# Fixed insertion plans for unit lists and row gathers, and two column groups for the last 64 undecided units

## The chip, the cores and the metric

One core of one Trainium2 chip runs the whole program: a block-recurrent cross attention whose output goes into a switch top-1 mixture of experts. The metric is the device time of the program in microseconds. Times inside the program (us from the start of the span) are those of one profiled execution.

## The reference, cut to what matters

```python
# attention: B=8, H=8, S=512, Ns=32, D=64
scores = scale * x @ state.T;   a  = softmax(scores);   xread = a @ state      # 512 token rows a batch
scores2 = scale * state @ x.T;  a2 = softmax(scores2);  sread = a2 @ x         # 32 state rows a batch
x = concat([xread, sread]) -> (B * (S + Ns), H * D) = (4352, 512)
# switch: E=8 experts, D=512, F=1024
expert_idx = argmax(x @ w_gate);  gate_w = softmax(x @ w_gate)[expert_idx]
out[rows of e] = gate_w * (relu(x[rows of e] @ w1[e]) @ w2[e])
```

Everything is float32.

## The kernel before, in words

The 512 token rows of a batch are taken to go to one expert, guessed from the mean of its states (table `eb`). A token row is a convex mixture of 32 state rows, so the kernel multiplies the states by w1 first (`states_w1` makes G, 32 x 1024 for each head) and bounds how far a token can lie from their mean. From that bound, `lists(b)` (7 steps) divides the 1024 hidden units of batch b in three kinds: units that are positive for every token (up to CAPP = 512; their relu does nothing, so they enter as one product M, matmuls `pm`), undecided units (up to CAPU = 192, as a group of 128 and one of 64; matmuls `phu`, relu into `hu`), and units that are never active, which are dropped.

A list goes this way. PE turns G (`pgt`), ACT copies it to `gt`, DVE takes statistics (`bn`) and computes row numbers (`nn` to `to`). POOL scatters the columns of G to their places in a DRAM table `g_dram` by 8 indirect DMAs. `fetch(b)` reads the sorted table back into `gp` by 3 DMAs, and `gather` fetches the matching rows of w2 by 6 indirect DMAs into `w2c`. `mask(b)` on DVE zeroes the places beyond the list's ends in `gp`. Then `batch(b)` runs on PE: `pgu` (turns the undecided units), `pm` (M), `phu`, and `py` in two pairs of chunks; ACT scales and stores. Batch 0 doesn't use lists: `in_full` computes all 1024 units.

The state rows (256, in two halves t = 0 and 1) are sorted by expert (`sort_states(t)`: matmuls `psT`, `pls`, `prs`, then about 41 small DVE instructions on 128x8 tables, here the sort chain) and computed in 3 rounds of 128 rows (`rounds`: the rows `xg` are read back from DRAM by POOL, then `ptx`, `pgh` twice, `pth`, `pgy` twice; weights come through a ring of 5 buffers of 0.786 MB, loaded four at a time).

Every engine runs its instructions in the order in which the program writes them. The order between the strands is set at insert points: `in_full` has 24 of them, and `batch` 13 (one behind `pgu`, four in `pm`, one behind each `phu`, three in each pair of `py`). A string at each point says which generators take a step: B `back` (second half of attention), T `front` (scores), S `lists`, F `fetch`, M `mask`, R the state rows, K late constants. Before, a generator whose turn came too early waited by its own `while ...: yield`; the list of batch b + 1 was scattered during batch b; fetch and its 6 gathers came together at insert point 10 of batch b (it needs `summed[0]`, set behind the last `pm`), and the mask right behind. The table `g_dram` was held twice, in turn.

Names in the rows and traces: every operation is recorded by one helper and so has the line L51; tiles tell them apart. A program matmul in float32 shows as two records.

Of the kernel before, what the change touches and what calls it, by code (L numbers as in the profile page):

```python
# [20 lines left out]
def kernel(  # L21
# [68 lines left out]

    st_dram = dram.tile([B * NS, DM], FP32)
    ss_dram = [dram.tile([NR * 128, XW], I32, name=f"ss_dram{t}") for t in range(NT)]
    g_dram = [dram.tile([CAPP + CAPU, GW], FP32, name=f"g_dram{i}") for i in range(2)]

    pa = ps_a.tile([128, 4, 512], FP32, name="pa")
    pc = pa[:, :, 0:256]
# [63 lines left out]
    gp.memset(blank2[:, DM + 1:DM + 2], FAR)  # L160

    def clear():
        for i in range(2):
            for r in range(0, CAPP + CAPU, 128):
                n = min(128, CAPP + CAPU - r)
                sp.dma_start(out=g_dram[i][ds(r, n)].bitcast(I32), in_=blank[0:n, 0:GW])
        for t in range(NT):
            for r in range(NR):
                sp.dma_start(out=ss_dram[t][ts(r, 128)], in_=blank2[:])
# [295 lines left out]
    def lists(b):  # L465

        G = new_G()
        w1t = w1s.pop(b)
        for k in range(2):
            states_w1(w1t, stT[:, 0, b], G, k)  # L470
            if k == 1 and b + 1 < B:
                load_next_w1(b + 1)
            yield
        gt = ffn.tile([128, NFC, GW], FP32, tag="gt", name="gt")
        dve.tensor_scalar(gt[:, :, GW - 1:GW].bitcast(I32), pos8[:].unsqueeze(2), e_at[:, b:b + 1], None, ALU.add)
        bn = ffn.tile([128, NFC, 2, 3], FP32, tag="bn", name="bn")
# [37 lines left out]
        for f in range(NFC):  # L514
            d = gp.indirect_dma_start(
                out=g_dram[b % 2][:], out_offset=bass.IndirectOffsetOnAxis(ap=to[:, f:f + 1], axis=0),
                in_=gt[:, f, :], in_offset=None, bounds_check=CAPP + CAPU - 1, oob_is_err=False)
            tc.declare_no_dep(d.ins, group=f"g{b}", reason="every unit has a row of its own")
            tc.add_to_no_dep_group(f"g{b}", d.ins)
        yield  # L520

    def fetch(b):

        t = gps[b] = ffn.tile([128, NP + NU, GW], FP32, tag="gp", bufs=2, name="gp")
        gp.dma_start(out=t[:, 0:NP + 1], in_=g_dram[b % 2][0:CAPP + 128].rearrange("(j p) k -> p j k", p=128))
        for u in range(2):
            gp.dma_start(out=t[ts(u, 64), NP + 1], in_=g_dram[b % 2][ds(CAPP + 128, 64)])
        w2cs[b] = []
        gather(b, NP + NU)

    def gather(b, n):
        rows = moe_w2.rearrange("e f d -> (e f) d")
# [20 lines left out]
    def batch(b, insert):  # L553
# [18 lines left out]
        for u in range(NU):  # L572
            ph = bank(name="phu")
            for g in range(2):
                pe.matmul(ph[:], lhsT=Gu[:, g, u, :], rhs=tokens_of(a)[:, g], start=(g == 0), stop=(g == 1))
            relu(hu[u][:], ph[:])
            insert()
        store = store_batch(b)
        for c0 in range(0, NC, 2):
# [5 lines left out]
                pe.matmul(py[i][:], lhsT=hu[0][:, ts(c0 + i, 128)], rhs=w2c[NP][:], start=False, stop=False)  # L585
                insert()
            for i in range(2):
                pe.matmul(py[i][:], lhsT=hu[1][ts(i, 64), ts(c0 + i, 128)], rhs=w2c[NP + 1][ts(i, 64)],
                          start=False, stop=True)
            for i in range(2):  # L590
                store(c0 + i, py[i])
# [187 lines left out]
    def late_constants():  # L779
# [2 lines left out]
        dve.tensor_copy(out=wt[:, 1:, 0], in_=eb[:, 1:])  # L782
        dve.tensor_tensor(wt[:, 1:, 1], eb[:, 1:], eb[:, 0:B - 1], ALU.not_equal)
        yield
        dve.tensor_scalar(U128[:], colf[:], iota_p[:, 0:1], None, ALU.is_gt)
        tmp = const.tile([128, 1], FP32)
        quad = const.tile([128, 1], FP32)
# [8 lines left out]
        dve.scalar_tensor_tensor(slot_u[:, 1:2], iota_p[:], 128.0, tmp[:], ALU.add, ALU.add)  # L796
        yield

    attended, done, summed, listed, fetched, turned = [0], [0], [0], [0], [0], [-1]

    def backs():
        for b in range(B):
            while done[0] < b - 3 or b not in soft:
                yield
            for _ in back(b):
                turned[0] = b
                yield
            attended[0] = b + 1

    def fronts():  # L810
        for b in range(1, B):
            for i, _ in enumerate(front(b)):
                yield
                while i == 1 and turned[0] < b - 1:
                    yield

    def listing():
        for b in range(1, B):
            for i, _ in enumerate(lists(b)):
                while (i == 5 and bounded[0] < b) or (i == 6 and fetched[0] < b - 2):  # L820
                    yield
                yield
            listed[0] = b
            yield

    def fetching():
        for b in range(1, B):
            while listed[0] < b or done[0] < b - 1 or summed[0] < b - 1:
                yield
            fetch(b)  # L830
            fetched[0] = b
            yield

    def masking():
        for b in range(1, B):
            while fetched[0] < b:
                for k in "BTSF":
                    next(todo[k], None)
            mask(b)
            yield  # L840

    def tokens():
        for t in range(NT):
# [25 lines left out]
    rest = ["S", "T", "B", "", "F", "B", "SBT", "ST", "SB", "SSM", "T", "ST", "S"]
    pieces = {1: (9, 10, 11, 12, 13), 2: (1, 6, 7, 12), 3: (3, 4, 8, 10, 13), 4: (4, 8, 9, 13),  # L870
              5: (9, 10, 11, 12, 13), 6: (1, 5, 6, 11), 7: (2, 3, 8)}
    for b in range(1, B):
        done[0] = b
        batch(b, inserts([k + "R" * pieces[b].count(i + 1) for i, k in enumerate(rest)]))
    for k in "BTSFMR":
        for _ in todo[k]:
            pass
# [133 lines left out]
```

## Time and profile before

| | |
|---|---|
| time, median of 3 runs | 451.41 us (444.86 to 452.32) |
| the profiled execution, its own time | 448.62 us |
| its span | 446.8 us |
| PE busy | 368.7 us, 83% |
| DVE busy | 206.2 us, 46% |
| ACT and POOL busy | 124.2 and 124.4 us, 28% each |
| DMA moved | 93.46 MB, mean 209 GB/s |

A row of the timeline gives the start, the length, the engine, the operation with output and inputs, and in brackets how long the engine was idle ahead of it and what it waited for. A matmul's form reads rows*columns of the array; 128*32 is one of four column groups. PEclk is the granted clock, 1.00 for the upper of the two levels and 0.50 for the lower. Batches begin at their `pgu`: 1 at 99.8, 2 at 148.2, 3 at 193.4, 4 at 251.4, 5 at 302.0, 6 at 346.4, 7 at 396.4.

### The profile page before, as it was taken

To read this page: it belongs to the slowest core of one execution; us is meant where nothing else is said; L and a number is where in the kernel's file an instruction comes from. 1 tells how busy PE (TensorE), PEld (TensorE's weight loads), DVE (VectorE), ACT (ScalarE), POOL (GpSimd) and SP (SyncE) were. 2 spreads that over 40 slices of the span, in tenths; PEclk is the share of its full clock that TensorE was granted. 3 is DMA by queue.
4 is the path that set the end of the run, shared out by engine and by line. 5 is a ranking of instruction groups with operands and counts; after the bars stand their busy time and mean duration, and the time that the engine had idled before them with its cause. 6 is when DMAs were issued, how large, how long until landed. Compare 5 with 4: busy or idle time off the path is not lost.

```text
span 446.8 us, 9127 instructions
## 1 busy us (share of the span) xinstructions
PE 368.7 (83%) x3288; PEld 168.4 (38%) x3288; DVE 206.2 (46%) x634; ACT 124.2 (28%) x226; POOL 124.4 (28%) x149
## 2 busy tenths in 40 slices
PE   4697999957994799869999699996999749729991
PEld 3443544433442454324523245342534323213330
DVE  4858697367528866490454706345123810010002
ACT  3623524114323341422322322430404211101110
POOL 2000006350155117250161603514073414431000
PEclk9899999986998599997999799997999888958998
DMA  6949982780254459687699944698024665878451
GB/s 182 384 154 252 273 295 70 240 293 28 69 160 130 128 167 292 220 289 269 234 292 377 366 143 139 226 331 301 5 74 134 188 227 213 262 265 254 156 209 76
DMA packets 51346, 93.46 MB, mean 209 GB/s; under 512 B 8583, under 2 KB 19538, under 8 KB 51296
## 3 DMA queue, kind: packets, MB, share of 16 engines
q1 hardware_dynamic: 37792, 61.76, 42.0%
q0 software_dynamic: 8368, 22.65, 15.6%
q10 hardware_dynamic: 5136, 8.41, 5.0%
q8 instruction: 28, 0.46, 0.4%
q14 instruction: 22, 0.18, 0.1%
HBM read 83.40 MB, written 21.15 MB: 234 GB/s over the span
## 4 chain that ended last, share of the span: by engine, by line
PE 32%; DMA 13%; issue 6%; DVE 3%; POOL 3%; ACT 2%; ACTq 0%; POOLq 0%
PE py L51 9%; PE pm L51 7%; DMA w2c<-in_moe_w_dram,gp 5%; PE pgh L51 4%; DMA gp<-g_dram 4%; PE phu L51 4%; PE pgy L51 3%; DMA g_dram<-gt,to 2%; POOL g_dram L51 2%; PE pa L51 1%; DMA xg<-ss_dram 1%; PE pG L51 1%; PE pw L51 1%; ACT y L51 1%; POOL gp L51 0%
## 5 line engine op out<-in xcount | busy, mean ns | idle before, releaser
L51 POOL DMA_INDIRECT g_dram<-gt,to x56 | 56.5, 1010 | 179.5 <-ACT a L51 65.6
L51 PE MATMUL pm<-w2c,gp 128*128 128x512 f32 x112 | 67.4, 745 | 15.6 <-DMA w2c<-in_moe_w_dram,gp 10.5
L51 POOL DMA_INDIRECT w2c<-in_moe_w_dram,gp x42 | 43.8, 1042 | 52.7 <-DMA gp<-g_dram 42.3
L51 PE MATMUL py<-M,aT 128*128 128x512 f32 x112 | 53.8, 603 | 0.0
L51 PE MATMUL py<-w2c,hu 128*128 128x512 f32 (+1 forms) x112 | 44.1, 617 | 0.0
L51 PEld LDWEIGHTS pm<-w2c,gp 128*128 128x128 f32 x112 | 24.0, 234 | 48.7 <-issue 36.5
L51 ACT ACTIVATE y<-py,gw 128x512 f32<-128x512 f32 x32 | 22.0, 689 | 51.1 <-PE py L51 43.4
L51 DVE TENSOR_SCALAR gp<-gp,mk 128x256 f32<-128x256 f32 x42 | 13.0, 367 | 45.8 <-DMA gp<-g_dram 45.7
L51 PEld LDWEIGHTS py<-M,aT 128*128 128x128 f32 x112 | 20.0, 189 | 24.8 <-issue 22.8
L51 PE MATMUL phu<-aT,Gu 128*128 128x512 f32 x56 | 28.4, 635 | 0.0
L51 PE MATMUL pgt<-ident,G 128*128 128x128 f32 x112 | 18.3, 287 | 10.1 <-ACT gt L51 6.1
L51 DVE BATCH_NORM_STATS2 bn<-gt 128x6 f32<-128x256 f32 x56 | 20.6, 412 | 12.4 <-ACT gt L51 12.4
L51 ACT COPY gt<-pgt 128x512 f32<-128x512 f32 x28 | 15.9, 589 | 35.9 <-PE pgt L51 28.2
L51 PE MATMUL pgh<-s,sxT 128*32 128x512 f32 x192 | 23.5, 633 | 1.8 <-ACT gt L51 1.8
L51 DVE TENSOR_SCALAR xs<-pw,s 128x64 f32<-128x64 f32 x16 | 3.8, 279 | 42.9 <-PE pw L51 42.9
L51 DVE COPY G<-pG 128x512 f32<-128x512 f32 x16 | 11.0, 689 | 25.5 <-PE pG L51 25.5
L51 PE MATMUL py<-s,s 128*128 128x512 f32 x48 | 22.5, 598 | 0.0
L51 PEld LDWEIGHTS py<-w2c,hu 128*128 128x128 f32 (+1 forms) x112 | 14.9, 187 | 19.0 <-issue 18.8
L51 PEld LDWEIGHTS pgt<-ident,G 128*128 128x128 f32 x112 | 12.8, 143 | 24.4 <-ACT gt L51 7.7
L51 POOL DMA_DIRECT2D gp<-g_dram x21 | 14.4, 696 | 26.8 <-issue 15.0
L51 PE MATMUL pgy<-s,shT 128*32 128x512 f32 x192 | 21.8, 595 | 0.0
L51 DVE STREAM_TRANSPOSE xt<-x_nat 128x1024 f32<-128x1024 f32 x16 | 19.4, 1228 | 2.4 <-DMA x_nat<-in_x_dram 2.4
(203 smaller groups left out, 473.7 us busy)
## 6 DMA issues: line engine op xcount, KB each, us to landing
s<-in_moe_w_dram SPq DMA_DIRECT2D x144, 256.0 KB
w1t<-in_moe_w_dram SPq DMA_DIRECT2D x8, 2048.0 KB
x_nat<-in_x_dram SPq DMA_DIRECT2D x16, 512.0 KB
out_dram<-y ACTq DMA_DIRECT2D x32, 256.0 KB
gp<-g_dram POOLq DMA_DIRECT2D x7, 642.5 KB, 7.2
ss_dram<-blank SPq DMA_DIRECT2D x8, 257.0 KB
s<-in_moe_w_dram SPq DMA_DIRECT2D x2, 768.0 KB
g_dram<-blank SPq DMA_DIRECT2D x10, 128.5 KB
```

The source lines that it names most:

```text
L51: ins = getattr(self.engine, name)(*args, **kw)
```

## The change

Every insert point now has a written string, in a table per batch (`plans`), and the waiting loops became asserts. Lists are made further ahead: the scatter of list b + 2 stands at insert point 12 of batch b where before that of b + 1 stood in batch b. Fetch and the gathers are three F steps (read the table back; 3 gathers; 3 gathers). One table `g_dram` is left of two. The clearing of the tables moved from before batch 0 behind the first load steps (a K step) and is 6 DMAs less. All rounds of state rows are over by batch 6. Separately, the 64-unit group of `phu`, which was computed 128 wide with each unit twice over 512 tokens (2 program matmuls), is now computed by 4 matmuls of 64 columns and 256 tokens in two column groups, each with half of the chunks, and its relu covers 256 columns instead of 512.

```diff
@@ -160,10 +160,9 @@
     def clear():
-        for i in range(2):
-            for r in range(0, CAPP + CAPU, 128):
-                n = min(128, CAPP + CAPU - r)
-                sp.dma_start(out=g_dram[i][ds(r, n)].bitcast(I32), in_=blank[0:n, 0:GW])
+        for r in range(0, CAPP + CAPU, 128):
+            n = min(128, CAPP + CAPU - r)
+            sp.dma_start(out=g_dram[ds(r, n)].bitcast(I32), in_=blank[0:n, 0:GW])
...
     def fetch(b):
 
         t = gps[b] = ffn.tile([128, NP + NU, GW], FP32, tag="gp", bufs=2, name="gp")
-        gp.dma_start(out=t[:, 0:NP + 1], in_=g_dram[b % 2][0:CAPP + 128].rearrange("(j p) k -> p j k", p=128))
+        gp.dma_start(out=t[:, 0:NP + 1], in_=g_dram[0:CAPP + 128].rearrange("(j p) k -> p j k", p=128))
...
         w2cs[b] = []
-        gather(b, NP + NU)
...
             ph = bank(name="phu")
             for g in range(2):
-                pe.matmul(ph[:], lhsT=Gu[:, g, u, :], rhs=tokens_of(a)[:, g], start=(g == 0), stop=(g == 1))
-            relu(hu[u][:], ph[:])
+                if u < NU - 1:
+                    pe.matmul(ph[:], lhsT=Gu[:, g, u, :], rhs=tokens_of(a)[:, g], start=(g == 0), stop=(g == 1))
+                else:
+                    for i in range(2):
+                        pe.matmul(ph[ts(i, 64), 0:S // 2].rearrange("p (c t) -> p c t", c=NC // 2), lhsT=Gu[:, g, u, ts(i, 64)],
+                                  rhs=a[:, g, i:NC:2].rearrange("p c i t -> p c (i t)"),
+                                  start=(g == 0), stop=(g == 1), skip_group_check=True)
+            n = S if u < NU - 1 else S // 2
+            relu(hu[u][:, 0:n], ph[:, 0:n])
...
-                pe.matmul(py[i][:], lhsT=hu[1][ts(i, 64), ts(c0 + i, 128)], rhs=w2c[NP + 1][ts(i, 64)],
+                pe.matmul(py[i][:], lhsT=hu[1][ts(i, 64), ts(c0 // 2, 128)], rhs=w2c[NP + 1][ts(i, 64)],
...
         dve.tensor_tensor(wt[:, 1:, 1], eb[:, 1:], eb[:, 0:B - 1], ALU.not_equal)
         yield
+        clear()
+        yield
...
     def backs():
         for b in range(B):
-            while done[0] < b - 3 or b not in soft:
+            assert done[0] >= b - 3 and b in soft
+            for i, _ in enumerate(back(b)):
+                turned[0], attended[0] = b, b + i // 3
                 yield
...
     def listing():
         for b in range(1, B):
             for i, _ in enumerate(lists(b)):
-                while (i == 5 and bounded[0] < b) or (i == 6 and fetched[0] < b - 2):
-                    yield
                 yield
-            listed[0] = b
-            yield
+                assert i != 5 or bounded[0] >= b
+                assert i != 6 or fetched[0] >= b - 1
 
     def fetching():
         for b in range(1, B):
-            while listed[0] < b or done[0] < b - 1 or summed[0] < b - 1:
-                yield
+            assert listed[0] >= b and summed[0] >= b - 2
             fetch(b)
             fetched[0] = b
             yield
+            assert done[0] >= b - 1
+            gather(b, 3)
+            yield
+            assert summed[0] >= b - 1
+            gather(b, 3)
+            yield
 
     def masking():
         for b in range(1, B):
-            while fetched[0] < b:
-                for k in "BTSF":
-                    next(todo[k], None)
+            assert fetched[0] >= b
             mask(b)
             yield
...
-    next(todo["B"])
+    for k in "BTT":
+        next(todo[k])
...
     load_next_w1(1)
-    clear()
     in_full(G, aTs[0], w2x, store_batch(0), inserts(
-        "TT,B,TK,BBT,TS,BS,BS,TTS,BS,TS,B,S,TS,T,B,S,BS,TT,F,BS,MTS,BS,TS,S".split(",")))
-    rest = ["S", "T", "B", "", "F", "B", "SBT", "ST", "SB", "SSM", "T", "ST", "S"]
-    pieces = {1: (9, 10, 11, 12, 13), 2: (1, 6, 7, 12), 3: (3, 4, 8, 10, 13), 4: (4, 8, 9, 13),
-              5: (9, 10, 11, 12, 13), 6: (1, 5, 6, 11), 7: (2, 3, 8)}
+        "T,BK,T,TK,BS,B,BS,BB,S,ST,S,S,S,ST,TB,TS,TS,BF,BT,FTS,BST,FSB,TS,TSM"))
+    plans = {
+        1: "SB,SB,S,B,FSBR,STR,STF,SR,TFR,STRM,T,S,BR",
+        2: "B,FS,SR,BTF,SBT,STR,ST,FSR,T,SR,BM,ST,BR",
...
+        6: ",F,R,F,,R,,F,,,M,,",
+        7: ",,,,,,,,,,,,",
+    }
```

On POOL around the end of batch 1 and into batch 2 (ss_dram is the sorted table of state rows, xg the rows read back of it, gp the list read back, w2c the gathered rows of w2), before:

```order
L51 DMA ss_dram_79<-srow,si 512x514
L51 DMA xg<-ss_dram_79 128x514
L51 DMA g_dram_82<-gt,to 704x257 x8
L51 DMA gp<-g_dram_82 128x5x257
L51 DMA gp<-g_dram_82 64x257 x2
L51 DMA w2c<-in_moe_w_dram,gp 128x512 x6
```

and of the change:

```order
L51 DMA ss_dram_79<-srow,si 512x514
L51 DMA g_dram<-gt,to 704x257 x8
L51 DMA xg<-ss_dram_79 128x514
L51 DMA gp<-g_dram 128x5x257
L51 DMA gp<-g_dram 64x257 x2
L51 DMA w2c<-in_moe_w_dram,gp 128x512 x6
```

The read of xg moved from ahead of a list's eight scatters to behind them.

On DVE at the edge from batch 1 to batch 2, where `mk` and `gp` are the masks of batch 2 (nm, sx, sm belong to a softmax, bn to a list's statistics, nn to a list's numbers; in the change `more` ends the sort chain of t = 0), before:

```order
L51 TENSOR_SCALAR mk<-slot_p,nn 128x4
L51 SCALAR_TENSOR_TENSOR mk<-slot_u,nn 128x2
L51 TENSOR_SCALAR gp<-gp,mk 128x256 x6
L51 TENSOR_REDUCE nm<-pa 128x2
L51 TENSOR_SCALAR nm<-nm 128x2
L51 BN_STATS bn<-gt 128x6 x2
L51 TENSOR_REDUCE sm<-sx 128x32
```

and of the change:

```order
L51 TENSOR_SCALAR more<-c_1773 128x1
L51 SCALAR_TENSOR_TENSOR more<-c_1774,more 128x1
L51 TENSOR_SCALAR mk<-slot_p,nn 128x4
L51 SCALAR_TENSOR_TENSOR mk<-slot_u,nn 128x2
L51 TENSOR_SCALAR gp<-gp,mk 128x256 x6
L51 TENSOR_REDUCE sm<-sx 128x32
L51 TENSOR_SCALAR sm<-sm 128x32
L51 RECIPROCAL sm<-sm 128x32
L51 TENSOR_TENSOR sx<-sx,sm 128x1024
L51 COPY nn<-rank 128x2
```

The masks of batch 2 stood ahead of the sort chain, and stand behind it now, with a softmax's second half and the next list's numbers behind them.

On PE at the same edge (pgu opens batch 2; pa_1896 and pa_1902 turn a2 of batch 4; ptx turns xg; prs ranks the state rows), before:

```order
L51 MATMUL pgu<-ident,gp 128x128 x4
L51 LDWEIGHTS U_337
L51 MATMUL prs<-oh,U_337 128x8
L51 LDWEIGHTS ones_b
L51 MATMUL prs<-oh,ones_b 128x8
L51 MATMUL pm<-w2c,gp 128x512 x4
```

and of the change:

```order
L51 MATMUL py<-w2c,hu 128x512 x2
L51 MATMUL pa_1896<-ident,a_1753 128x128 x4
L51 MATMUL pa_1902<-ident,a_1753 128x128 x4
L51 MATMUL pgu<-ident,gp 128x128 x4
L51 MATMUL pw<-x_nat,a2T 32x64 x32
L51 MATMUL pl<-aT,gst 32x128 x8
L51 MATMUL pm<-w2c,gp 128x512 x2
L51 MATMUL pG<-w1t,stT 32x512 x8
L51 MATMUL pm<-w2c,gp 128x512 x2
L51 MATMUL pG<-w1t,stT 32x512 x8
L51 MATMUL ptx<-ident,xg 128x128 x4
```

`prs` moved from behind pgu to well ahead of it (py, rank and the turns of a2 lie between); pw, pl and pG of later batches now lie among the pm, and ptx behind the second of them.

## Rows read from the trace of the kernel before

**Rows 1.** Timeline, PE, 98 to 152: start us, us, work [idle before <-releaser].

```profile
99.77 1.11 PE L51 MATMUL pgu<-ident,gp 128*128 128x128 f32 x4 [4.66 <-DVE cnt L51]
104.20 2.08 PE L51 MATMUL pm<-w2c,gp 128*128 128x512 f32 x2 [3.31 <-ACT gt L51]
...
145.73 1.12 PE L51 MATMUL pgt<-ident,G 128*128 128x128 f32 x4 [6.14 <-ACT gt L51]
...
151.22 0.19 PE L51 MATMUL prs<-oh,U 128*128 128x8 bf16 x1 [1.92 <-DVE oh L51]
```

**Rows 2.** Waits of PE from 190 to 405: us in total, times, longest.

```profile
PE pm L51 <- DMA w2c<-in_moe_w_dram,gp: 10.5, 5, 4.4
PE pgu L51 <- DVE gp L51: 8.7, 2, 8.5
PE ptx L51 <- DMA xg<-ss_dram: 6.2, 1, 6.2
PE prs L51 <- DVE oh L51: 2.9, 1, 2.9
PE pgt L51 <- DVE ys L51: 2.7, 1, 2.7
```

**Rows 3.** Sum of five windows after 190: length, PE busy (granted clock 0.50 in each).

```profile
sum 37.55, PE 27.55; mean PE 5.51
```

**Rows 4.** Timeline, POOL, one list of units (the third).

```profile
168.68 1.00 POOL L51 DMA_INDIRECT g_dram<-gt,to  x1 [6.32 <-DVE r L51]
...
183.80 2.06 POOL L51 DMA_DIRECT2D gp<-g_dram  x3 [4.97 <-issue]
189.13 1.10 POOL L51 DMA_INDIRECT w2c<-in_moe_w_dram,gp  x1 [3.27 <-DMA gp<-g_dram]
...
193.16 1.81 POOL L51 DMA_INDIRECT w2c<-in_moe_w_dram,gp  x1 [0.30 <-PE py L51]
...
196.58 1.00 POOL L51 DMA_INDIRECT w2c<-in_moe_w_dram,gp  x1 [0.30 <-issue]
```

**Rows 5.** Waits of POOL over the whole program.

```profile
POOL g_dram L51 <- ACT a L51: 65.6, 1, 65.6
...
POOL w2c L51 <- DMA gp<-g_dram: 42.3, 8, 9.6
```

**Rows 6.** Timeline, DVE, 107 to 113: second half of one batch's softmax.

```profile
107.99 1.20 DVE L51 TENSOR_REDUCE sm<-sx 128x32 f32<-128x1024 f32 x1
...
111.09 1.25 DVE L51 STREAM_TRANSPOSE aT<-sx 128x1024 f32<-128x1024 f32 x1
```

**Rows 7.** Timeline, DVE, 344 to 359: the masks, then the sort chain's ends.

```profile
344.99 1.95 DVE L51 TENSOR_SCALAR gp<-gp,mk 128x256 f32<-128x256 f32 x6 [4.38 <-DMA gp<-g_dram]
...
351.75 0.14 DVE L51 CAST wi<-prs 128x8 int32<-128x8 f32 x1
...
358.59 0.16 DVE L51 SCALAR_TENSOR_TENSOR more<-c,more 128x1 f32<-128x1 f32 x1
```

**Rows 8.** Timeline, PE, 163 to 241: prices of PE steps at full clock.

```profile
163.40 1.10 PE L51 MATMUL pw<-x_nat,a2T 128*32 128x64 f32 x64
...
175.20 1.09 PE L51 MATMUL pG<-w1t,stT 64*32 64x512 f32 x16
...
217.72 1.98 PE L51 MATMUL phu<-aT,Gu 128*128 128x512 f32 x4
...
237.37 3.64 PE L51 MATMUL pgy<-s,shT 128*32 128x512 f32 x32
```

**Rows 9.** Page, DMA issues: KB each, median us from issue to landing.

```profile
xg<-ss_dram POOLq DMA_DIRECT2D x3, 257.0 KB, 5.0
```

**Rows 10.** Windows by stage: length, busy (x) of PE, PEld, DVE, ACT, POOL, PEclk, DMA, GB/s.

```profile
193.40:251.40 58.00, 49.24 (x442) 20.87 (x441) 27.10 (x70) 16.05 (x29) 16.97 (x18) 0.94 0.87 301
...
396.40:446.80 50.40, 39.05 (x164) 14.10 (x164) 5.46 (x20) 6.79 (x11) 7.12 (x7) 0.87 0.51 171
```

**Rows 11.** Timeline, DVE, 438 to 441: the last of the count behind the rows.

```profile
440.57 0.15 DVE L51 CAST rest_i<-rest_f 128x1 int32<-128x1 f32 x1
```

More of the change, by code (lines that the diff above doesn't have):

```diff
@@ L92 @@
     ss_dram = [dram.tile([NR * 128, XW], I32, name=f"ss_dram{t}") for t in range(NT)]
-    g_dram = [dram.tile([CAPP + CAPU, GW], FP32, name=f"g_dram{i}") for i in range(2)]
+    g_dram = dram.tile([CAPP + CAPU, GW], FP32, name="g_dram")
     pa = ps_a.tile([128, 4, 512], FP32, name="pa")
@@ L515, in lists @@
             d = gp.indirect_dma_start(
-                out=g_dram[b % 2][:], out_offset=bass.IndirectOffsetOnAxis(ap=to[:, f:f + 1], axis=0),
+                out=g_dram[:], out_offset=bass.IndirectOffsetOnAxis(ap=to[:, f:f + 1], axis=0),
                 in_=gt[:, f, :], in_offset=None, bounds_check=CAPP + CAPU - 1, oob_is_err=False)
@@ L519, in lists @@
             tc.add_to_no_dep_group(f"g{b}", d.ins)
+        listed[0] = b
         yield
@@ L524, in fetch @@
         t = gps[b] = ffn.tile([128, NP + NU, GW], FP32, tag="gp", bufs=2, name="gp")
-        gp.dma_start(out=t[:, 0:NP + 1], in_=g_dram[b % 2][0:CAPP + 128].rearrange("(j p) k -> p j k", p=128))
+        gp.dma_start(out=t[:, 0:NP + 1], in_=g_dram[0:CAPP + 128].rearrange("(j p) k -> p j k", p=128))
         for u in range(2):
-            gp.dma_start(out=t[ts(u, 64), NP + 1], in_=g_dram[b % 2][ds(CAPP + 128, 64)])
+            gp.dma_start(out=t[ts(u, 64), NP + 1], in_=g_dram[ds(CAPP + 128, 64)])
         w2cs[b] = []
-        gather(b, NP + NU)
     def gather(b, n):
@@ L802, in backs @@
         for b in range(B):
-            while done[0] < b - 3 or b not in soft:
+            assert done[0] >= b - 3 and b in soft
+            for i, _ in enumerate(back(b)):
+                turned[0], attended[0] = b, b + i // 3
                 yield
-            for _ in back(b):
-                turned[0] = b
-                yield
-            attended[0] = b + 1
     def fronts():
@@ L813, in fronts @@
                 yield
-                while i == 1 and turned[0] < b - 1:
-                    yield
+                assert i != 1 or turned[0] >= b - 1
     def listing():
@@ L819, in listing @@
             for i, _ in enumerate(lists(b)):
-                while (i == 5 and bounded[0] < b) or (i == 6 and fetched[0] < b - 2):
-                    yield
                 yield
-            listed[0] = b
-            yield
+                assert i != 5 or bounded[0] >= b
+                assert i != 6 or fetched[0] >= b - 1
     def fetching():
         for b in range(1, B):
-            while listed[0] < b or done[0] < b - 1 or summed[0] < b - 1:
-                yield
+            assert listed[0] >= b and summed[0] >= b - 2
             fetch(b)
@@ L843, in tokens @@
         for t in range(NT):
-            while attended[0] < 4 * (t + 1):
-                yield
+            assert attended[0] >= 4 * (t + 1)
             yield from sort_states(t)
@@ L851, in inserts @@
     def inserts(plan):
-        steps = iter(plan)
+        steps = iter(plan.split(","))
         def insert():
             for k in next(steps):
-                next(todo[k], None)
+                next(todo[k])
         return insert
-    next(todo["B"])
+    for k in "BTT":
+        next(todo[k])
     G = [sst.tile([128, F], FP32, tag=n, name="G0") for n in ("sh", "shT")]
@@ L865 @@
     load_next_w1(1)
-    clear()
     in_full(G, aTs[0], w2x, store_batch(0), inserts(
-        "TT,B,TK,BBT,TS,BS,BS,TTS,BS,TS,B,S,TS,T,B,S,BS,TT,F,BS,MTS,BS,TS,S".split(",")))
-    rest = ["S", "T", "B", "", "F", "B", "SBT", "ST", "SB", "SSM", "T", "ST", "S"]
-    pieces = {1: (9, 10, 11, 12, 13), 2: (1, 6, 7, 12), 3: (3, 4, 8, 10, 13), 4: (4, 8, 9, 13),
-              5: (9, 10, 11, 12, 13), 6: (1, 5, 6, 11), 7: (2, 3, 8)}
+        "T,BK,T,TK,BS,B,BS,BB,S,ST,S,S,S,ST,TB,TS,TS,BF,BT,FTS,BST,FSB,TS,TSM"))
+    plans = {
+        1: "SB,SB,S,B,FSBR,STR,STF,SR,TFR,STRM,T,S,BR",
+        2: "B,FS,SR,BTF,SBT,STR,ST,FSR,T,SR,BM,ST,BR",
+        3: "B,FS,SBTR,TF,ST,SR,ST,FSR,B,STR,BMT,ST,B",
+        4: "BT,FS,STR,BF,SB,SBR,SB,FSR,R,SR,M,SR,R",
+        5: "R,FS,SR,F,S,SR,S,FSR,,SR,M,S,R",
+        6: ",F,R,F,,R,,F,,,M,,",
+        7: ",,,,,,,,,,,,",
+    }
     for b in range(1, B):
         done[0] = b
[L874 to L877, printed above, removed]
+        batch(b, inserts(plans[b]))
+    for k, left in todo.items():
+        assert next(left, None) is None, k
     others = const.tile([128, B, E], FP32)
```

## The prediction

> **What bounds the kernel now.** I read first where the matmul engine stands idle, then at what clock it works, then what DVE and POOL do just before. PE's timeline shows runs of dense work, and a few long holes where one batch ends and the next begins. At 0→1 it waits 4.66 ahead of pgu and 3.31 ahead of the first pm; at 1→2, 6.14 and 1.92: 8.06 [rows 1]. From 190 to 405 PE's waits by what ended them are 10.5 (gathered rows), 8.7 (masks), 6.2 (xg), 2.9 (route of the state rows) and 2.7 (a state result): 31.0, of which 24.8 without xg's [rows 2]. Each hole is followed by work at half clock. Five windows of it after 190, xg's left out, hold 27.55 of PE work; at full clock that would take half, so they cost 13.8 [rows 3]. The reader is to see that a hole is paid about one and a half times.
>
> What makes those late holes is POOL's chain for one list: 8 scatters (168.68 to about 178.8), 4.97 until the fetch, 2.06 to issue it, 3.27 until its rows are there, 6 gathers from 189.13 to 197.6 [rows 4]. PE opened batch 3 at 193.4 and so met the gathers half done. The chain is serial, about 29 us, and its start is late: before the fetch at point 10 it may not go on.
>
> **The change part by part.** I make the sum against the profiled execution's own time, 448.6, which is 2.8 below the median of 451.4.
>
> *Edges from 2→3 on: −24.8 and −13.8.* A list is scattered a batch ahead of its fetch, the fetch stands at point 2 or 4 of the batch before, the gathers at points 2 to 8, and the mask at point 11. Laid along PE's work by those points, the rows land some 20 us ahead of pgu in batches 3 and 4, 6 to 12 in 5 and 6, and about with it in 7, where I leave 1.5 of waiting (below). A wait for the fetch of 9.6, the longest seen [rows 5], where the list shown has 3.27, would take up what is spare in 5 alone. So the waits on gathers, masks and results go, and the half clock behind them. What hides the chain now is a whole batch of PE work (50 to 58 [rows 10]); if that cover were gone, the old holes would be back. xg's wait in batch 6 I leave in: t = 1's rows are sorted and read back in one go in batch 5 as they were in 6.
>
> *Column groups: −6.0.* A phu group of four records takes 1.98 with the end of its last, so about 0.43 a record, 1.72 in all [rows 8]. With 64 columns and 256 tokens in each half of the array the same product needs half: 0.86 saved in each of 7 batches. That column groups run side by side is seen in this trace: 32 records of pgy, four column groups of 32, take 3.64, where 32 times 0.43 would be 13.8 [rows 8]. Bounds: 0 (one after the other) and 6.0; I take 6.0, since the groups of pgy overlap fourfold. The relu is shorter on an engine that doesn't bind.
> The Trainium skill (TensorEngine Tiling (Array Packing), Key Properties) says that a change of tiling mode drains the engine. Of pgy the row shows 3.64 against 8 times 0.43, 3.44 [rows 8], thus up to 0.2 for a mode's end; two more such changes a batch would take back 7 × 0.4 = 2.8 by that rule, and I leave it out of the sum.
>
> *Batch 0: −2.* The clearing writes no longer stand ahead of the loads of x, and the 3.31 ahead of pm [rows 1] goes, since the rows of list 1 are landed by then. The mask of batch 1 now stands last on DVE behind a softmax, so a wait ahead of pgu stays, 4.66 or more. Bounds −4 (all of it gone but that) and +3 (the softmax steps ahead of the masks, at 1.2 each, all late); I take −2, since the 3.31 is the surer part.
>
> *Edge 1→2: +2.4.* The order on DVE is now: sort chain, masks, softmax end, numbers of list 3, aT; before, the masks were first. The chain is 351.75 to 358.75, 7.0; masks with their two marks 2.35 [rows 7]: 9.35 from prs to pgu, while PE has some 7.1 of py, rank and turns there. That is a wait of 2.4 if the chain starts right at prs and of 6.2 if a list's statistics (13 small steps at about 0.2) and a reduction of 1.2 [rows 6] stand ahead of it; I take 4.4. Then pl waits for aT: four softmax steps 3.0, six numbers 1.0, aT 1.25 [rows 6], 5.2 against 1.6 of PE (pgu and pw [rows 8]), so 3.7. prs itself waits for the route, 1.92 and 2.9 before [rows 1, 2]; 2.4. Together 10.5 in place of 8.06.
>
> *xg in batch 2: +10.* Before, xg was read before the scatters of list 3, and ptx found it there. Now it stands behind them on POOL. From the end of the masks (T): numbers ready T + 4.1; eight scatters of 1.27 (168.68 to 178.83 [rows 4]) end T + 14.4; xg issued and landed (5.0, [rows 9]) T + 20. PE gets to ptx at about T + 11.3 (pl at 5.4 and 0.44 long, then four records of pm twice 1.72, pG twice 1.03 [rows 8]). Wait 8.6, and 1.4 for the clock behind it. Everything on PE after ptx in the batch (pm, pgt, phu) waits with it. Bounds: 5 (the scatters go earlier) and 12.
>
> *Rounds closer together: +3.* The two halves of pgh now stand some 4.3 apart in a batch, with only five ring buffers; a half needs four more, 3.1 MB, which at 301 GB/s [rows 10] is 10.4, from the first release 2.7 before the end of the first half. I take 1 for each of three rounds; bounds 0 and 4.
>
> *Smaller:* scores of batch 7, which stood under the old holes, +2.6 (two softmax steps of 1.20 and 1.25, [rows 6], and their start); prs in batch 5, which I removed with the late edges, comes back, +2.4; the rows of batch 7, +1.5. At the tail, the last state result and a dozen small instructions up to rest_i (440.57 [rows 11]) stand no longer behind the last matmul: a dozen times 0.17 (41 in 7.0 [rows 7]) and one of 0.75, −2.8; bounds 0 and −4.
>
> Sum: −24.8 − 13.8 − 6.0 − 2.0 + 2.4 + 10 + 3 + 2.6 + 2.4 + 1.5 − 2.8 = −27.5, so 421.1. Of PE's small waits of under 0.75 I assume that they stay.
>
> **Rivals.**
> *(a) The forecast*, late edges close and early ones don't: about 421, 407 to 432 by the bounds of its terms.
> *(b) Early edges close too.* The first two edges (4.66 + 3.31 + 8.06 [rows 1]) and the added waits (10 + 2.4 + 3 + 2.6 + 2.4 + 1.5 = 21.9) come from where DVE and POOL stand, by a few microseconds each. If DVE keeps up (it is busy 27 of 58 in the densest stretch [rows 10]) half of these 38 goes, 19, and some 4 of half clock behind it: about 398. Against it: in batch 1 the order on DVE leaves no room.
> *(c) Waits move.* The same transfers now fall into fewer microseconds, and rounds, gathers and lists of three batches share DMA at 0.87 of its time in one stretch already [rows 10]. If each late edge keeps half of its hole (38.6/2), 421.1 + 19.3 = 440. For it: the row of 193 to 251; against it: after batch 5 nothing is left to fetch.
> *(d) The column groups don't run side by side:* 421.1 + 6 = 427, the part of the change that does not do what it says.
> *(e) Slower.* With one table, scatter of list b + 1 may start only behind the fetch of list b, so POOL's chain cannot overlap itself. If the cycle of a list is C, POOL, which starts on its first list near 69 (65.6 of it waiting [rows 5]), ends its last gather near 69 + 7C, and 50.4 of batch 7 follow [rows 10]; that exceeds the span of 446.8 from C = 46.8. At C = 50 the time is 471. From the rows C is 29, with the longest wait 9.6 [rows 5] 35; POOL would have to be held 12 a list longer. It's a little chance.
> *(f) POOL's own issue slows.* One gather took 1.81 where others take 1.00 [rows 4]. If DVE work, denser now, did that to each of the 14 indirect DMAs of a list, 0.8 × 14 = 11 a cycle: it would eat the 6 to 12 that 5 and 6 have spare and come out in full at 7: some 5 and 11, 437.
> The Trainium skill (SBUF — State Buffer, section SBUF: two separate sides) has the rule behind (f): a DVE copy in a two-port mode locks GpSimd out of writing descriptors. [...]
>
> **How the numbers follow.** Chances: (a) 0.50, (b) 0.20, (c) 0.13, (d) 0.08, (e) 0.04, (f) 0.05. The predicted time is that of (a), 421. The range reaches from 394, a little under (b)'s 398 since its half could be more, to (c)'s 440: 394 to 440 leaves out (e), and the ends of (b) and (c), some 2 in 10. (a)'s own range is 407 to 432. About 2% (9 us of 451) is what a measurement of this kernel can tell from no change. Faster by over 2% means under 442.4: (a), (b), (d), (f) and most of (c), 0.88. Within 2%: the rest of (c) and of (f), 0.08. Slower: (e), 0.04.
>
> **What would show it.** In the profile after: no wait of PE for w2c, none of pgu for masks from batch 3 on, no low clock there but around the ptx of the second half; phu's second group at about 0.9; in batch 2 a wait of ptx for xg of 5 to 12, in batch 1 waits of prs, pgu and pl that add to some 10; on POOL a fetch that starts more than 25 before its pgu. Wrong if PE still stops for w2c or masks in batches 4 to 7 (c, e, f), if phu's group takes 1.7 (d), or if ptx in batch 2 finds its rows (b).

## The result, and the profile after

| | before | after |
|---|---|---|
| median | 449.28 us (4 runs, 444.86 to 452.32) | 427.24 us (4 runs, 427.11 to 428.27) |
| ratio to before | | 0.9546, 95% interval 0.9456 to 0.9636 |
| the profiled execution, its own time | 448.62 us | 427.33 us |
| its span | 446.8 us | 425.5 us |

The change is faster by 4.5%; forecast were 421 and a range of 394 to 440. Ratios leave out a run that took over 1.5% more than the fastest of its kernel: here the 452.32, and below one of 441.3 among the runs with later lists. The page of the changed kernel, busy times and the granted clock in 40 slices:

```profile
PE 363.0 (85%) x3316; PEld 166.4 (39%) x3316; DVE 205.4 (48%) x634; ACT 122.5 (29%) x226; POOL 125.0 (29%) x149
...
PEclk9989999996997966999999899999998698999998
```

The span lost 21.3: PE's busy time 5.7 (368.7 to 363.0) and PE's idle time 15.6. PE's waits from 190 on in the changed kernel (us in total, times, longest), the answer to [rows 2]:

```profile
PE ptx L51 <- DMA xg<-ss_dram: 9.3, 1, 9.3
PE phu L51 <- ACT M L51: 3.2, 1, 3.2
PE pgh L51 <- DMA s<-in_moe_w_dram: 2.2, 1, 2.2
...
PE pgy L51 <- DMA s<-in_moe_w_dram: 0.9, 2, 0.7
PE prs L51 <- DVE oh L51: 0.8, 1, 0.8
```

No wait for gathered rows and none for masks is left there; 10.5 and 8.7 stood there before. What is left is a wait for xg, one behind ACT, and waits for the weights of the state rounds, which the kernel before did not have. The long waits one by one, PE's timeline (in brackets the idle time ahead and what it waited for):

```profile
102.01 1.12 PE L51 MATMUL pgu<-ident,gp 128*128 128x128 f32 x4 [8.03 <-issue]
...
135.24 0.19 PE L51 MATMUL prs<-oh,U 128*128 128x8 bf16 x1 [3.23 <-DVE oh L51]
...
152.58 1.08 PE L51 MATMUL pl<-aT,gst 128*32 128x128 f32 x16 [4.45 <-DVE s L51]
...
167.84 1.09 PE L51 MATMUL ptx<-ident,xg 128*128 128x128 f32 x4 [6.67 <-DMA xg<-ss_dram]
...
237.54 1.08 PE L51 MATMUL phu<-aT,Gu 128*64 128x256 f32 x8 [3.23 <-ACT M L51]
...
333.55 1.08 PE L51 MATMUL ptx<-ident,xg 128*128 128x128 f32 x4 [9.27 <-DMA xg<-ss_dram]
```

The first edge costs what it cost (8.03 in one piece, 4.66 + 3.31 before [rows 1]); the second too (3.23 + 0.51 ahead of pgu + 4.45 = 8.19 against 8.06). The two ptx waits stand where xg was put behind a list's scatters on POOL.

### The profile page after: what moved, and what is told of

It is laid out like the page before. It is cut to its first block, busy times and chain, and to the rows that moved or that the text cites. A ratio compares the mean times of both kernels' runs of the same rounds, so it can differ in the third digit from the quotient of the medians.

```text
span 425.5 us, 9174 instructions
## 1 busy us (share of the span) xinstructions
PE 363.0 (85%) x3316; PEld 166.4 (39%) x3316; DVE 205.4 (48%) x634; ACT 122.5 (29%) x226; POOL 125.0 (29%) x149
## 3 DMA queue, kind: packets, MB, share of 16 engines
q1 hardware_dynamic: 36992, 61.04, 44.0%
## 5 line engine op out<-in xcount | busy, mean ns | idle before, releaser
L51 POOL DMA_INDIRECT g_dram<-gt,to x56 | 56.3, 1004 | 177.0 <-DVE to L51 93.8
L51 PE MATMUL py<-M,aT 128*128 128x512 f32 x112 | 58.6, 649 | 0.0
L51 PE MATMUL pm<-w2c,gp 128*128 128x512 f32 x112 | 56.4, 636 | 2.2 <-ACT y L51 1.5
L51 POOL DMA_INDIRECT w2c<-in_moe_w_dram,gp x42 | 44.6, 1062 | 43.7 <-DMA gp<-g_dram 33.1
L51 PEld LDWEIGHTS py<-M,aT 128*128 128x128 f32 x112 | 21.4, 207 | 27.7 <-issue 25.8
L51 PEld LDWEIGHTS pm<-w2c,gp 128*128 128x128 f32 x112 | 20.9, 202 | 28.6 <-issue 23.3
L51 PE MATMUL pgh<-s,sxT 128*32 128x512 f32 x192 | 25.9, 600 | 2.2 <-DMA s<-in_moe_w_dram 2.2
L51 PE MATMUL pgy<-s,shT 128*32 128x512 f32 x192 | 26.1, 596 | 1.5 <-DMA s<-in_moe_w_dram 0.9
L51 PE MATMUL phu<-aT,Gu 128*64 128x256 f32 (+1 forms) x84 | 21.8, 486 | 3.2 <-ACT M L51 3.2
L51 PE MATMUL pa<-xt,stT 32*32 32x128 f32 x1024 | 18.9, 295 | 4.1 <-DVE xt L51 3.2
L51 PE MATMUL pG<-w1t,stT 64*32 64x512 f32 x256 | 19.6, 634 | 0.6 <-DVE G L51 0.6
L51 DVE STREAM_TRANSPOSE sx<-pa 128x256 f32<-128x256 f32 x32 | 11.5, 417 | 17.8 <-PE pa L51 17.8
L51 DVE COPY G<-pG 128x512 f32<-128x512 f32 x16 | 10.9, 688 | 17.3 <-PE pG L51 17.3
```

Source lines behind the costliest of these rows:

```text
L51: ins = getattr(self.engine, name)(*args, **kw)
```

## The experiments

Times are medians of four runs, beside runs of the kernel before on the same chip (450.6 for the first four experiments, 450.3 for the three after them). The changed kernel stood at 427.2 (427.1 to 428.3), and on the chip of those three at 427.4 (424.6 to 429.4). It was not run again beside the first four, where the kernel before took 450.6 for the result's 449.3, so of their differences from it only the 4.4 of the third round lies clear of the scatter.

**The column groups undone.**

```diff
-                if u < NU - 1:
-                    pe.matmul(ph[:], lhsT=Gu[:, g, u, :], rhs=tokens_of(a)[:, g], start=(g == 0), stop=(g == 1))
-                else:
-                    for i in range(2):
-                        pe.matmul(ph[ts(i, 64), 0:S // 2].rearrange("p (c t) -> p c t", c=NC // 2), lhsT=Gu[:, g, u, ts(i, 64)],
-                                  rhs=a[:, g, i:NC:2].rearrange("p c i t -> p c (i t)"),
-                                  start=(g == 0), stop=(g == 1), skip_group_check=True)
-            n = S if u < NU - 1 else S // 2
-            relu(hu[u][:, 0:n], ph[:, 0:n])
+                pe.matmul(ph[:], lhsT=Gu[:, g, u, :], rhs=tokens_of(a)[:, g], start=(g == 0), stop=(g == 1))
+            relu(hu[u][:], ph[:])
...
-                pe.matmul(py[i][:], lhsT=hu[1][ts(i, 64), ts(c0 // 2, 128)], rhs=w2c[NP + 1][ts(i, 64)],
+                pe.matmul(py[i][:], lhsT=hu[1][ts(i, 64), ts(c0 + i, 128)], rhs=w2c[NP + 1][ts(i, 64)],
```

> The changed kernel with its second phu group as before: 128 wide over 512 tokens, 2 program matmuls, the relu over 512 columns. If the two column groups run side by side and PE's own work is what the time is made of, 7 times 0.75 to 0.86 comes back: 432.5 to 433.5 against 427.2. If the column groups save nothing (one after the other) or the saving only goes into waits that follow, the time stays within 1 us of 427.

Measured: 429.9 (427.3 to 432.0), 2.7 over the changed kernel, by runs that scatter over 4.7; the ratio to the kernel before, 0.954, is that of the changed kernel, 0.955. The group itself, first in this kernel, where the next step starts 1.82 behind it, then in the changed kernel, 1.02:

```profile
185.40 1.98 PE L51 MATMUL phu<-aT,Gu 128*128 128x512 f32 x4
187.22 0.60 PE L51 MATMUL pgt<-ident,G 128*128 128x128 f32 x4
```

```profile
182.96 1.08 PE L51 MATMUL phu<-aT,Gu 128*64 128x256 f32 x8
183.98 0.66 PE L51 MATMUL pgt<-ident,G 128*128 128x128 f32 x4
```

Side by side they do run: 0.80 saved seven times is 5.6 of PE's work. How much of it is in the time isn't settled by these runs. That a part goes into waiting for the weights of pgh behind it is possible, but not shown: pgh is busy for 24.1 here and for 25.9 and 25.4 in two traces of the changed kernel, pgy for 26.3 against 26.1 and 27.2.

**Fetch and gathers back at point 10.**

```diff
-        2: "B,FS,SR,BTF,SBT,STR,ST,FSR,T,SR,BM,ST,BR",
+        2: "B,S,SR,BT,SBT,STR,ST,SR,T,FFFSRM,B,ST,BR",
```

(batches 1 to 6 alike)

> The changed kernel, lists still scattered a batch ahead, but the reading back of the table and all six gathers stand together at insert point 10 of the batch before, as in the kernel before, with the mask right behind. If the gain is that rows are gathered early, the holes ahead of pm and pgu at the edges from 2 to 3 on come back (24.8 us of waits and 13.8 us at low clock in the kernel before; part of it stays away since the scatters are over, so about two thirds of it): 445 to 460. If the gain comes from the lists alone, or from the other moves of the plan, the time stays near 430.

Measured: 429.4 (428.5 to 431.5), 2.2 over, and the ratio to the kernel before is again 0.955. The holes do not come back. POOL's timeline tells why; here the fetch and the first gather for batch 3, first with them at point 10, then in the changed kernel, with fetch at point 2 and gathers at points 4 and 8:

```profile
166.85 2.01 POOL L51 DMA_DIRECT2D gp<-g_dram  x3 [4.63 <-issue]
172.33 1.08 POOL L51 DMA_INDIRECT w2c<-in_moe_w_dram,gp  x1 [3.47 <-DMA gp<-g_dram]
```

```profile
166.46 2.02 POOL L51 DMA_DIRECT2D gp<-g_dram  x3 [3.84 <-issue]
172.31 1.09 POOL L51 DMA_INDIRECT w2c<-in_moe_w_dram,gp  x1 [3.82 <-DMA gp<-g_dram]
```

The same microsecond. An insert point fixes the order on each engine, not a time: POOL has nothing else to do there, does not wait for PE's point, and goes on when the scatters have landed. That is so for batch 3. For batches 4 to 7 the fetch does come 6 to 16 later with point 10, since other work stands ahead of it on POOL, such as the store of a state round. The fetch for batch 5, first with point 10, then in the changed kernel:

```profile
297.49 0.97 POOL L51 DMA_INDIRECT out_dram<-ys,xg  x1 [22.45 <-DVE c_sq L51]
298.45 2.07 POOL L51 DMA_DIRECT2D gp<-g_dram  x3
```

```profile
282.53 2.07 POOL L51 DMA_DIRECT2D gp<-g_dram  x3 [6.05 <-DMA g_dram<-gt,to]
```

Even so PE waits only once after 190 for gathered rows, and never for masks:

```profile
PE pm L51 <- DMA w2c<-in_moe_w_dram,gp: 0.6, 1, 0.6
```

With the list scattered a batch ahead, the later fetches still have room. Splitting F in three steps and moving it ahead bought nothing that these runs can tell.

**The lists four list steps later.** List b + 1 is scattered in the middle of batch b, as in the kernel before; fetch and gathers at point 10, masks at 11.

```diff
-        2: "B,FS,SR,BTF,SBT,STR,ST,FSR,T,SR,BM,ST,BR",
+        2: "B,S,SR,BT,SBT,STR,ST,SR,T,FFFSR,MB,ST,BR",
...
-        6: ",F,R,F,,R,,F,,,M,,",
+        6: ",S,SR,,S,SR,,,,FFF,M,,",
```

(four S steps left out in batch 1 and put into batch 6, so that every later list step comes four S steps later)

> The changed kernel with every list step four steps later (list b + 1 scattered in the middle of batch b), fetch and gathers at point 10, masks at 11. If the early scatter is what closed the late edges, 15 us or more slower than the changed kernel on the same chip, with waits of pm for gathered rows and of pgu for masks at the edges; if the order of the rest did it, within 6 us of it.

Measured: 436.1 (434.7 to 436.9), ratio to before 0.971 (0.962 to 0.980); 8.7 over the changed kernel on the same chip. PE's waits from 190 on:

```profile
PE pm L51 <- DMA w2c<-in_moe_w_dram,gp: 8.0, 5, 3.0
PE pgh L51 <- DMA s<-in_moe_w_dram: 5.3, 3, 4.2
PE pgu L51 <- DVE gp L51: 2.9, 1, 2.9
...
PE ptx L51 <- DMA xg<-ss_dram: 1.1, 1, 1.1
```

Between the two expectations. The waits for gathered rows and masks are back, 10.9 of the 19.2 of before. At the same time ptx has lost nearly all of its waits (1.1 after 190, none in batch 2, against 9.3 and 6.7), because later scatters leave POOL free for xg. So early lists are worth the holes (some 11 here), and cost the two waits of ptx. The 8.7 is not the price of the holes alone: pgh grows, too, from 25.4 busy and 1.5 of waiting for weights in the changed kernel on this chip to

```profile
L51 PE MATMUL pgh<-s,sxT 128*32 128x512 f32 x192 | 32.1, 618 | 6.6 <-DMA s<-in_moe_w_dram 6.5
```

This run also holds the edit of the one before, with fetch and gathers at point 10, which by itself was not told from nothing.

**xg of the first round ahead of list 3's scatters.**

```diff
-        1: "SB,SB,S,B,FSBR,STR,STF,SR,TFR,STRM,T,S,BR",
+        1: "SB,SB,S,B,FSBR,STR,STF,SR,TFR,STRM,T,R,BS",
```

> The changed kernel, with the reading back of the sorted state rows (xg of the first round) issued on POOL ahead of list 3's eight scatters and not behind them: points 12 and 13 of batch 1 change places. If the order on POOL is what ptx in batch 2 waits for, its wait of 6.67 us goes, with 1.2 us of the low clock behind it: 419 to 421. If the wait only moves (to the weights, to DVE), the time stays above 424.

Measured: 424.8 (422.2 to 427.9), 2.4 less, which is within the scatter. Waits of PE from 140 to 200 (the profiled execution is the one of 427.9):

```profile
PE pl L51 <- DVE s L51: 3.7, 1, 3.7
PE pgh L51 <- DMA s<-in_moe_w_dram: 2.6, 2, 1.8
```

The wait of ptx (6.67) is gone from the list, so the order on POOL was its cause. But little or nothing of it is in the time, as the second of the expectations had it: pgh, which now begins 5.6 earlier, waits 2.6 for weights, and its second group goes from 182.01 to 192.30, 10.3 where it took 5.24 in the changed kernel.

**The third round half a batch later.**

```diff
-        5: "R,FS,SR,F,S,SR,S,FSR,,SR,M,S,R",
-        6: ",F,R,F,,R,,F,,,M,,",
+        5: "R,FS,SR,F,S,S,S,FS,,S,M,S,R",
+        6: "R,F,R,F,,R,,FR,,R,M,,",
```

> The changed kernel, with the round of the second half of the state rows moved: ptx at point 13 of batch 5 instead of 6, and the steps behind it at points 1, 3, 6, 8 and 10 of batch 6, which has no waits of its own. If the 9.27 us that ptx waits in batch 5 and the 2.2 us that pgh waits for weights are only a matter of where these steps stand, they go, with the low clock behind them (2 to 3 us): 413 to 417. If the DMA engines were the limit there, the waits appear in batch 6 instead and the time stays above 423.

Measured: 422.8 (422.5 to 423.0), 4.4 less, where 10 to 14 were expected. The 9.27 are gone (ptx in batch 2, which the edit leaves alone, waits 8.30 here); in batch 6 the timeline has instead:

```profile
344.14 5.34 PE L51 MATMUL pgh<-s,sxT 128*32 128x512 f32 x32 [2.86 <-ACT sxT L51]
...
353.04 5.03 PE L51 MATMUL pgh<-s,sxT 128*32 128x512 f32 x32
...
379.72 3.16 PE L51 MATMUL pgy<-s,shT 128*32 128x512 f32 x8 [1.54 <-DMA s<-in_moe_w_dram]
```

A group of 32 took 3.64 in the kernel before (pgy in [rows 8]) and takes 5.34 and 5.03 here. A part of the first ran at the low clock; the second ran at 1.00 throughout. Gaps inside such a group are too small to be told as waits, and show as its length.

**A third of the weights.** Both last experiments point at the weights, so their load was taken away.

```diff
+    for s in rings:
+        gp.memset(s[:, 2], 0.0)
...
-                    for q in range(3):
+                    for q in range(1):
                         src = (moe_w1[ds(ex[r][q], 1), ts(k, 128), ts(half, 512)] if kind == 1
```

> The changed kernel with a third of the state rounds' weights loaded (the state rows come out otherwise). If late weights stretch pgh and pgy and the DMA load delays xg, 8 to 15 us faster than the changed kernel on the same chip, pgh and pgy back to some 21.4 us each at full clock; if changes of matmul form stretch them, or nothing waits for these loads, within 3 us.

Measured: 410.0 (409.3 to 412.6), 17.4 under the changed kernel on the same chip. The hardware queue that carries them moved 40.06 MB for 61.04. The two pgh groups of the first round, first with a third of the weights, then in the changed kernel:

```profile
177.38 3.64 PE L51 MATMUL pgh<-s,sxT 128*32 128x512 f32 x32
...
185.56 3.64 PE L51 MATMUL pgh<-s,sxT 128*32 128x512 f32 x32
```

```profile
179.39 3.64 PE L51 MATMUL pgh<-s,sxT 128*32 128x512 f32 x32
...
187.58 5.24 PE L51 MATMUL pgh<-s,sxT 128*32 128x512 f32 x32
```

And over all groups, page 5, with a third of the weights, then in the changed kernel (busy, mean ns | idle before):

```profile
L51 PE MATMUL pgy<-s,shT 128*32 128x512 f32 x192 | 21.8, 595 | 0.7 <-ACT G L51 0.5
L51 PE MATMUL pgh<-s,sxT 128*32 128x512 f32 x192 | 21.8, 595 | 0.0
```

```profile
L51 PE MATMUL pgh<-s,sxT 128*32 128x512 f32 x192 | 25.9, 600 | 2.2 <-DMA s<-in_moe_w_dram 2.2
L51 PE MATMUL pgy<-s,shT 128*32 128x512 f32 x192 | 26.1, 596 | 1.5 <-DMA s<-in_moe_w_dram 0.9
```

Of the 17.4, 8.4 are in these two groups, 2.2 + 0.9 in waits before them; ptx waits 4.5 and 7.1 instead of 6.7 and 9.3. Late weights it is, not changes of form: the order of matmuls is the same in both kernels.

**All of it in another order.** Masks of batch 1 and 2 ahead of softmax and sort chain; the first sort chain behind aT; xg ahead of fetch; state rounds spread up to batch 7.

```diff
-        "T,BK,T,TK,BS,B,BS,BB,S,ST,S,S,S,ST,TB,TS,TS,BF,BT,FTS,BST,FSB,TS,TSM"))
+        "T,BK,T,TK,BS,B,BS,BB,S,ST,S,S,S,ST,TB,TS,TS,BF,BT,FTS,BST,FSBM,TS,TS"))
...
-        1: "SB,SB,S,B,FSBR,STR,STF,SR,TFR,STRM,T,S,BR",
-        2: "B,FS,SR,BTF,SBT,STR,ST,FSR,T,SR,BM,ST,BR",
-        3: "B,FS,SBTR,TF,ST,SR,ST,FSR,B,STR,BMT,ST,B",
+        1: ",B,SB,SB,SFBR,STR,STF,SR,SFRT,MST,T,BS,R",
+        2: "B,RFS,S,BTF,SBT,ST,ST,FSR,T,S,BMR,ST,B",
+        3: "B,FSR,SBTR,TF,ST,SR,ST,FSR,B,STR,BMT,STR,B",
...
-        6: ",F,R,F,,R,,F,,,M,,",
-        7: ",,,,,,,,,,,,",
+        6: ",FR,,F,,,R,FR,,,MR,,",
+        7: ",,,,,R,,,,,,,",
```

> The changed kernel with the masks of batch 1 and 2 ahead of softmax and sort chain, the first sort chain behind aT, xg ahead of fetch, and the rounds spread evenly up to batch 7. In the disturbed call pgh and pgy took 43.4 us at full clock in it and no ptx waited for xg. If these waits are a matter of order, 12 to 25 us faster than the changed kernel on the same chip; if DVE's work in batch 1 and the DMA's rate are the bound, less than 6.

Measured: 396.4 (395.6 to 397.6), ratio to before 0.880 (0.873 to 0.886); 31 under the changed kernel on the same chip, more than the 12 to 25 expected. It is the fastest of all the kernels here. Its page, and PE's waits from 90 to 390:

```profile
PE 351.8 (89%) x3309; PEld 161.1 (41%) x3316; DVE 205.9 (52%) x634; ACT 122.6 (31%) x226; POOL 123.6 (31%) x149
...
PEclk9989999999999979999899899999999999999999
```

```profile
PE pgy L51 <- DMA s<-in_moe_w_dram: 3.9, 1, 3.9
PE pq L51 <- ACT sq L51: 3.4, 1, 3.4
PE pa L51 <- ACT a L51: 3.3, 1, 3.3
PE rank L51 <- DVE marks L51: 2.0, 1, 2.0
```

No ptx waits, pgu of batch 1 starts at 93.25 instead of 102.01, and no wait in this stretch is as long as 4. The clock falls less: its mean over the execution is 0.977, for 0.935 in the changed kernel on this chip. The granted-clock row has no slice under 0.7; in the changed kernel five slices stand at 0.6 or 0.7 between 95 and 345. DVE does the same work (205.9 against 205.4): its amount was never the bound, its order was. Which of the four moves brought how much was not tried.

**Four runs that can't be used.** The last three of these kernels ran first on another chip, where the kernel before took 468 us, with one more: the kernel before with the column groups alone.

> The changed kernel with every step of the lists four list steps later, so that list b + 1 is scattered in the middle of batch b as in the kernel before, and with fetch and the six gathers at point 10 and the mask at 11; everything else (rounds, softmaxes, column groups) stands as in the changed kernel. If it is the lists' early scatter that closed the late edges, the holes come back at the edges from 2 to 3 on, 24.8 us of waits and some 10 us of low clock: 450 to 465. If the gain came from the order of the rest (rounds, softmaxes) or from where fetch and gathers stand, the time stays under 435.

> The changed kernel, with one third of the state rounds' weights loaded (one expert's part of each ring buffer and not three; the others hold what was there, so the state rows come out otherwise). 144 loads become 48, up to 25 MB less. If pgh and pgy are stretched by weights that are late (they take 7.5 us more of PE's time than in the kernel before, and wait 2.9 besides), and the rows xg land late because of them, that goes, and a part of the 16 us of ptx waits: 410 to 417. If changes between forms of matmul stretch them, the time stays above 423.

> The kernel before with the two column groups alone: 64 columns by 256 tokens for the second phu group, its relu over 256 columns. If the saving on PE adds up wherever it stands, 2.7 (what it is worth in the changed kernel) to 6.0 us less than before: 444.5 to 448 against 450.5. If the holes at the edges take it up, since they end when POOL's chain ends, the time does not move by 1 us.

> The changed kernel with other plans: the masks of batch 1 and 2 ahead of the softmax and the sort chain, the sort chain of the first state rows behind aT, xg ahead of fetch, the rounds spread evenly up to point 6 of batch 7. If the waits that are left (8.0 ahead of pgu of batch 1, 8.2 at the edge to batch 2, ptx 6.7 and 9.3, weights some 10, and 13 of low clock) come from the order on DVE and POOL, half of these 55 us goes: 395 to 408. If they come from DVE's work or from the DMA's rate, they only move, and the time stays above 418.

Measured: 472.8, 460.6, 449.3 and 448.1, beside 468.1 for the kernel before. Two rows of the last kernel show what is wrong with them: PE issues two small matmuls every 1.4 us, and ACT and PE stand still for several us on something outside the program:

```profile
168.08 0.33 PE L51 MATMUL pw<-x_nat,a2T 128*32 128x64 f32 x2 [1.09 <-issue]
```

```profile
129.17 0.59 ACT L51 COPY G<-pG 128x512 f32<-128x512 f32 x1 [7.37 <-remote]
```

64 of these pw matmuls take 1.10 in the kernel before [rows 8]. The trace with the column groups alone has such stops as well (8.2 us ahead of pa that nothing explains). I draw nothing from these four. So what the column groups are worth alone stays open.

The changed kernel ran once more on the chip of the last three experiments above (late lists, a third of the weights, another order), as what they are measured against:

> The changed kernel once more, on the same chip as the three behind it. In the call before this one the kernel before took 468 us where it had taken 450, and PE stood for some 16 to 32 us without a reason that the trace shows; this run is what the others are compared with. On a chip like the first ones: 426 to 429.

Measured: 427.4 (424.6 to 429.4).

## Why the prediction was right, and where its steps were off

The sign and the range held, and the likeliest case was (a): late edges close, early ones don't. 427.3 for the profiled execution is 6.2 above the 421.1 of the sum. That it is so near is in part luck: by the list below, terms came out some 19 worse than the sum had them and others some 8 better. Term by term:

- **Late edges, −24.8.** All of those waits went, and no wait of more than 0.9 at a later batch's start took their place. **The reason given was wrong in one half.** The step said that rows land early because fetch and gathers stand at points 2 to 8, and that before "the fetch at point 10 it may not go on". With fetch at point 10, POOL fetches for batch 3 at the same microsecond and for batches 4 to 7 6 to 16 later, and the holes stay closed all the same. What counts is when the list is scattered: four list steps later, 10.9 of 19.2 are back. What closed the rest isn't shown.
- **Low clock, −13.8 there and +1.4 at xg.** **Mis-sized by some 3.5.** PE's busy time times what the granted clock lacks to 1.00, added up over stretches of 2 us (an estimate from the profile's windows), is 15.9 after 190 before and 5.6 in the changed kernel: −10.3. Ahead of 190 it goes from 8.6 to 9.4. After 190 the low clock does not lie around ptx alone, as forecast: it is there also behind phu's wait of 3.23 and behind a wait of 2.19 for the weights of pgh, two waits that the sum did not have.
- **Column groups, −6.0.** 0.80 a batch, 5.6 of PE's work, near the forecast; of the kernel's time 2.7, which is less than its runs scatter by, so the 6.0 is neither shown nor refuted there. The rule of the Trainium skill (TensorEngine Tiling (Array Packing), Key Properties), that a change of tiling mode drains the engine, has little room: the group takes 1.02, where half of 1.82 would be 0.91, so some 0.1 a batch.
- **Batch 0, −2, was not there.** The wait ahead of pgu became 8.03, as long as both waits before together, because the mask stood behind a softmax on DVE; the kernel in another order, with the mask ahead of it, starts batch 1 8.8 earlier.
- **Edge 1→2, 10.5.** 8.19: prs 3.23 (2.4), pgu 0.51 (4.4), pl 4.45 (3.7). The order on DVE was read rightly, and DVE was as late as the step feared, with its first mask 10.3 behind prs. That pgu waits only 0.51 is luck: PE had 10.2 of work there and not 7.1, since the py behind the wait of prs ran at the low clock (four records in 3.76 for 1.88):

```profile
135.31 3.76 PE L51 MATMUL py<-M,aT 128*128 128x512 f32 x4
...
140.23 1.88 PE L51 MATMUL py<-M,aT 128*128 128x512 f32 x4
...
146.00 0.97 PE L51 MATMUL pgu<-ident,gp 128*128 128x128 f32 x4 [0.51 <-ACT y L51]
```

```profile
145.55 1.88 DVE L51 TENSOR_SCALAR gp<-gp,mk 128x256 f32<-128x256 f32 x6
```

- **xg in batch 2, a wait of 8.6.** 6.67. Cause shown by moving xg.
- **Rounds closer together, +3, was mis-sized.** pgh and pgy grew from 23.5 and 21.8 busy to 25.9 and 26.1, part of pgh's 23.5 at low clock, and waits of 3.1 came to it. A third of the weights gives 17.4 back, which is more than this term, since it also takes away load that the kernel before had. The sum had one wait of 1 a round, worked out from one half's four buffers with the mean of 301 GB/s as if they had the DMA to themselves. It should have set a whole round's 12.6 MB, 42 us at that mean, against the 41 to 54 us that a round has here from its first pgh to its last pgy, beside lists, x and w1; in the kernel before it had 53 to 72.
- **ptx of the second half, left at 6.2.** 9.27: POOL has list 6's scatters and the fetch ahead of it there, as it has list 3's scatters in batch 2. I looked for that in one batch alone.
- **Smaller.** phu waits 3.23 in batch 3 for ACT, which evicts M behind a softmax: not foreseen. prs in batch 5 0.76 (2.4), batch 7's rows 0 (1.5), its scores 1.49 (2.6). The tail: PE's last group starts at 417.27 and takes 2.08, so 6.1 is left to the end where 8.9 was: −2.8, as forecast.

Of the rivals, (b) did not come true in this kernel, but the kernel in another order shows that its mechanism was real: order on DVE and POOL, with the state rounds spread out, was worth another 31. How the 31 divide between them was not tried. (c) is there in part, with the weights, not with the lists. (d) and (e) did not show. For (f), the page has 1004 and 1062 ns for the two kinds of indirect DMA where it had 1010 and 1042, with DVE at 48%:

```profile
L51 POOL DMA_INDIRECT g_dram<-gt,to x56 | 56.3, 1004 | 177.0 <-DVE to L51 93.8
...
L51 POOL DMA_INDIRECT w2c<-in_moe_w_dram,gp x42 | 44.6, 1062 | 43.7 <-DMA gp<-g_dram 33.1
```

What (f) feared is there all the same, but rare. Three of these 98 take 1.84 to 2.00, and each of the three starts under one DVE operation, a TENSOR_TENSOR over sx of 128x1024 with two inputs, and ends 0.85 to 0.91 behind it; the 1.81 of [rows 4] lies under one as well (192.88 to 194.10). One of them:

```profile
90.50 1.93 POOL L51 DMA_INDIRECT w2c<-in_moe_w_dram,gp  x1 [0.31 <-issue]
```

```profile
90.34 1.23 DVE L51 TENSOR_TENSOR sx<-sx,mx 128x1024 f32<-128x1024 f32 x1
```

That agrees with the rule of the Trainium skill (SBUF — State Buffer, section SBUF: two separate sides) that a DVE operation with two SBUF inputs and a GpSimd operation that reads SBUF contend for a shared port pair, and the one that starts first shuts the other out until it ends. It costs POOL some 2.8 in the whole program.

## What to carry to other kernels

A place in the program's order is not a time: before a step is credited with being issued earlier, look at what its own engine's queue waits for, and move that. When work is packed closer, set the bytes that it needs against the time that it gets, over the whole round; and look at the length of groups, not only at their waits. And price a wait with the clock behind it: here even the 3.23 ahead of prs were followed by py at half the clock, and 2.19 ahead of pgh likewise.

## What was not expected of the hardware

Late operands can hide inside a group of matmuls: the same 32 records took 3.64 or 5.24 with no wait told ahead of them. An indirect DMA that POOL starts under a TENSOR_TENSOR of 1.2 us on DVE took up to 2.00 for 1.00. And one chip ran the kernel before at 468 us where others took 450; the traces kept from it have engines at a standstill that no instruction of the program explains.
